# Weight sums, activation differences and output stores: three rearrangements in a fused attention and two-network kernel

## The chip, the cores and the metric

The kernel runs on one core of a Trainium2 chip. The metric is the device time of one launch in microseconds (us), as the median of several runs.

## The reference

```
a    = softmax(scale * q @ k^T, causal) @ v
mem  = (phi(q) @ M_prev) / (phi(q) . z_prev + 1e-6)      phi(x) = elu(x) + 1
x    = sigmoid(beta) * mem + (1 - sigmoid(beta)) * a     -> 2304 tokens x 512
h    = x @ moe_w_in            512 x 2048
x    = (h * cos(h)) @ moe_w_out
h    = x @ moe2_w_in
out  = (h * tanh(softplus(h))) @ moe2_w_out              -> 2304 x 512
```

Everything is float32, with 4 batches, 8 heads, 576 positions and 64 values a head. h * tanh(softplus(h)) is the Mish function.

## The kernel before

TensorE works on pairs of numbers: each float32 operand is split into a rounded upper half (H) and the remainder (L), and a product is three matmuls, H by H, H by L and L by H. Whoever makes an operand makes a rounded copy and then subtracts it from the original; that subtraction is called the remainder below.

The work has four stages. In the first, attention runs in 80 steps (batch, head pair, block of queries), and beside it the first half of the first network: products with w_in (L428) in 256 columns, the cosine, its remainders gL on Pool (L400), products with w_out (L494). The second stage, from some 405 us, is the second half of the first network with 512 columns. The third and last is the second network as a Strassen product: three blocks of 768 tokens, in each of them eight groups of 256 hidden units, so 24 groups. A group has seven products with w_in (`product`, L771) into three PSUM banks A, B, C, which are added up on the way: x1 is a copy of the first product by ScalarE (L786), `add` (L669, VectorE) adds x1 or a sum to a bank, `act` (L673, ScalarE) is Mish. From the four activations r11, r12, r21 and r22, `sub` makes four differences. `t1` and `t2` are new tiles and are made on VectorE (L662); the other two overwrite r12 and r21 in place and are made on Pool (L664), by the last group on VectorE. `halves` rounds each of the seven operands on ScalarE (L130) and makes its remainder on Pool (L680). `last_products` multiplies the operands of two groups at a time by sums of w_out (L744); `done` adds each to a sum in SBUF (L710), and at the last pair of groups of a token block combines the seven sums by additions that go to VectorE and Pool in turn (L704, L721) and stores the results (L708).

The Strassen network needs sums of weights, which `strassen_weights` makes for 16 pieces: sums and differences on Pool (L560), rounded copies on ScalarE (L130), remainders on Pool or VectorE in turn (L566) and a store to DRAM (L567). Six pieces are made beside attention, by a generator `gi` of which each attention step from 29 to 79 takes one turn. The other ten are made beside the second half of the first network by `gc`, one or two turns for each unit of that network; `strassen_x` makes sums of the input beside it in the same way (L584, L591, L605, L607). `load_w` (L620) brings the sums back, on the queue of SyncE (SP), where output stores are issued as well.

The program is written stage by stage. A scheduler of the language orders the instructions of each engine by its own estimate of the time; the engines then run in that order, each one waiting at an instruction until its operands are there. `tc.issue_after(x)` tells the scheduler that what follows may not be placed ahead of instruction x; `marks` holds the last instruction of a kind, and `TURNS` the engines that a kind of work goes to in turn ("p" Pool, "v" VectorE, "a" ScalarE).

```
halves(k, "S3", sub(r22, r12, r12, k + 1 == n))
halves(k, "A22", sub(t2, r21, r21, k + 1 == n))
...
with tc.issue_after(marks["cos"]), tc.issue_after(last_sin[0]):
    for _ in range(1 if i % SUM2 == 0 else 2):
        next(gc, None)
```

## Time and profile before

| | |
|---|---|
| runs shown | 1056.64, 1059.21, 1059.36 us, median 1059.21 |
| profiled execution | 1057.27 us, of which 1055.5 us are the span of the trace |
| granted TensorE clock, mean of the span | 0.986 |
| busy: TensorE, VectorE, ScalarE, Pool | 96%, 64%, 55%, 60% of the span |

The span runs from the first instruction to the last; busy time is the time in which an engine executes an instruction, so an engine that waits counts as idle. In rows of the trace PE is TensorE, DVE is VectorE, ACT is ScalarE, POOL is Pool and SP is SyncE, and L400 is line 400 of the kernel.

### The profile page before, as it was taken

The page shows a single profiled execution, that of the slowest core. Times are in us where ns is not written, and L with a number is a line of the kernel's source. Part 1 is how long each engine was busy: PE and PEld are TensorE (multiplying, and loading weights), DVE is VectorE, ACT ScalarE, POOL GpSimd, SP SyncE. Part 2 cuts the span into 40 slices and gives each one's busy share as a digit, 9 for nine tenths or more (in the row PEclk, how much of TensorE's full clock was granted, in tenths as well). Part 3 has the DMA queues.
Part 4 walks back from the last instruction along what each step waited for, and adds up shares of the span by engine and source line. Part 5 has one row for each costly group of instructions (what it writes and reads, how often), then busy time and mean ns, then how long its engine had stood idle before and what let it go on. Part 6 is the DMA issues. An engine that isn't in the chain of part 4 may idle for free.

```text
span 1055.5 us, 19374 instructions
## 1 busy us (share of the span) xinstructions
PE 1017.3 (96%) x6704; PEld 897.9 (85%) x6704; DVE 673.5 (64%) x1400; ACT 576.1 (55%) x1274; POOL 634.7 (60%) x623
## 2 busy tenths in 40 slices
PE   6998999999999999999999989998999999999997
PEld 4665678887878889998887878898999899999996
DVE  3589866667565645885495876453597347962557
ACT  5787576758576653334365555456444454445441
POOL 3368754454444533555386687279677767786664
PEclk8999799999999999999999999999999999999999
DMA  7377554636342247435268989996977888797882
GB/s 255 130 217 243 176 196 145 208 100 232 120 166 104 80 146 269 160 101 170 98 236 291 325 298 335 406 329 246 380 268 256 262 289 293 237 310 237 276 282 80
DMA packets 121841, 236.19 MB, mean 224 GB/s; under 512 B 11920, under 2 KB 35984, under 8 KB 121744
## 3 DMA queue, kind: packets, MB, share of 16 engines
q1 hardware_dynamic: 121744, 234.95, 65.2%
q8 instruction: 54, 0.88, 0.3%
q14 instruction: 43, 0.35, 0.1%
HBM read 176.44 MB, written 58.46 MB: 223 GB/s over the span
## 4 chain that ended last, share of the span: by engine, by line
PE 67%; DMA 9%; DVE 9%; ACT 6%; POOL 4%; issue 4%; SPq 1%; POOLq 0%; ACTq 0%; DVEq 0%
PE y L744 15%; PE h L771 15%; PE h L428 12%; PE y L494 11%; PE o L339 4%; PE sp L252 4%; PE tp L312 3%; DMA wst<-in_w1i_dram 2%; DMA wst<-in_w1o_dram 2%; PE o L328 1%; DVE wst L146 1%; DMA w<-woD 1%; DMA wsD<-ws 1%; POOL at L279 1%; DMA woD<-ws 1%
## 5 line engine op out<-in xcount | busy, mean ns | idle before, releaser
L494 PE MATMUL y<-g,w 128*128 128x256 f32 (+1 forms) x1344 | 222.4, 318 | 4.9 <-POOL g L400 3.9
L680 POOL TENSOR_TENSOR g<-us,g 128x384 fp32r<-128x384 f32 x164 | 177.3, 1099 | 74.2 <-ACT g L130 73.0
L494 PEld LDWEIGHTS y<-g,w 128*128 128x128 f32 x1344 | 191.3, 190 | 33.5 <-issue 10.3
L428 PE MATMUL h<-xbH,w 128*128 128x256 f32 (+1 forms) x896 | 206.5, 318 | 0.6 <-DMA xbH<-xsH 0.6
L744 PE MATMUL y<-g,w 128*128 128x384 f32 x1008 | 196.2, 336 | 4.0 <-DMA w<-woD 2.5
L771 PE MATMUL h<-xc,wq 128*128 128x384 f32 x1008 | 195.7, 335 | 2.6 <-ACT us L786 2.5
L279 POOL TENSOR_SCALAR at<-at,sm,omg 128x128 f32<-128x128 f32 (+2 forms) x144 | 114.3, 802 | 115.2 <-DVE sm L277 68.0
L744 PEld LDWEIGHTS y<-g,w 128*128 128x128 f32 x1008 | 175.9, 188 | 7.2 <-DMA w<-woD 2.4
L771 PEld LDWEIGHTS h<-xc,wq 128*128 128x128 f32 x1008 | 176.2, 188 | 3.4 <-ACT us L786 2.8
L400 POOL TENSOR_TENSOR g<-u,g 128x512 fp32r<-128x512 f32 x72 | 103.3, 1449 | 111.7 <-ACT g L130 54.5
L428 PEld LDWEIGHTS h<-xbH,w 128*128 128x128 f32 x896 | 151.3, 192 | 12.9 <-DMA xbH<-xsH 1.0
L428 PE MATMUL h<-xbL,w 128*128 128x256 f32 (+1 forms) x448 | 141.3, 316 | 0.0
L669 DVE TENSOR_TENSOR us<-h,us 128x384 f32<-128x384 f32 x120 | 66.3, 554 | 109.6 <-PE h L771 78.7
L130 ACT ACTIVATE g<-us 128x384 fp32r<-128x384 f32 x168 | 86.4, 523 | 57.1 <-DVE us L662 29.9
L428 PEld LDWEIGHTS h<-xbL,w 128*128 128x128 f32 x448 | 85.9, 192 | 5.3 <-issue 0.3
L673 ACT ACTIVATE us<-us 128x384 f32<-128x384 f32 x72 | 37.6, 524 | 96.1 <-DVE us L669 96.1
L257 ACT ACTIVATE at<-at,mn 128x128 f32<-128x128 f32 (+3 forms) x128 | 71.0, 556 | 26.1 <-DVE mn L254 24.4
L382 ACT ACTIVATE u<-h 128x512 int32<-128x512 f32 x72 | 42.0, 591 | 71.1 <-PE h L428 70.9
L710 DVE TENSOR_TENSOR ac<-y,ac 128x384 f32<-128x384 f32 x120 | 63.8, 550 | 22.1 <-PE y L744 21.7
L254 DVE CUSTOM_DVE_ANT_0 at<-sp,mask 128x128 f32<-128x128 f32 (+3 forms) x128 | 59.5, 483 | 25.5 <-PE sp L252 20.5
L312 PE MATMUL tp<-ident,at 128*128 128x128 f32 x384 | 65.5, 289 | 9.6 <-POOL at L279 6.0
L383 DVE SCALAR_TENSOR_TENSOR u<-u,h 128x512 f32<-128x512 int32 x72 | 48.3, 679 | 39.5 <-ACT u L382 39.4
(106 smaller groups left out, 1561.5 us busy)
## 6 DMA issues: line engine op xcount, KB each, us to landing
wq<-wsD SPq DMA_DIRECT2D x168, 256.0 KB, 4.5
w<-woD SPq DMA_DIRECT2D x168, 256.0 KB, 4.7
wsD<-ws SPq DMA_DIRECT2D x24, 512.0 KB, 3.2
woD<-ws SPq DMA_DIRECT2D x24, 512.0 KB, 4.4
wst<-in_w1i_dram SPq DMA_DIRECT2D x16, 512.0 KB, 4.5
wst<-in_w1o_dram SPq DMA_DIRECT2D x16, 512.0 KB, 4.8
wst<-in_w2i_dram SPq DMA_DIRECT2D x16, 512.0 KB, 4.5
wst<-in_w2o_dram SPq DMA_DIRECT2D x16, 512.0 KB, 5.2
```

Source lines behind the costliest of these rows:

```text
L130: eng.activation(dst, src, AF.Copy, scale=scale)
L257: marks["act"] = nc.scalar.activation(at[:, :N], at[:, :N], AF.Exp, bias=mn[:, j:j + 1], scale=-1.0, accum_out=sm[:, j:j + 1]).ins
L279: marks["pool"] = turn_of("sc", b == 0).tensor_scalar(at[:, :N], at[:, :N], sm[:, j:j + 1], gates[j], ALU.mult, ALU.mult).ins
L312: nc.tensor.transpose(tp[:, c:c + P], at[:, c:c + P], ident)
L400: turn_of(kind).tensor_tensor(gL, g, gH.bitcast(F32), ALU.subtract)
L428: nc.tensor.matmul(h[:, a * T:(a + 1) * T], w_[:, c, f0:f0 + P], x_[c], start=m == 0, stop=m == 3 * NC - 1)
L494: nc.tensor.matmul(y[e // per][:, cols], w_[:, f, es], g_, start=fst and m == 0 and e % per == 0, stop=lst and m == 2, skip_group_check=True)
L669: marks['v'] = nc.vector.tensor_tensor(c, b, x, ALU.add).ins
L680: ins = turn_of("ml" if k + 1 < n else "mz").tensor_tensor(t[:, 1], x, t[:, 0].bitcast(F32), ALU.subtract).ins
L710: marks['v'] = nc.vector.tensor_tensor(a, *((a, y) if less else (y, a)), ALU.subtract if less else ALU.add).ins
L744: nc.tensor.matmul(y, w_[:, wl, c], x[:, xl], start=m == 0, stop=m == 3 * KS - 1, skip_group_check=True)
L771: nc.tensor.matmul(b, w[name][:, wl, c], x[name][:, xl, c], start=first and m == 0, stop=m == 5, skip_group_check=True)
```

## The change

It makes five edits. (1) The turns of `gi` beside attention begin six steps later in the constant (SUM0 38, first turn at step 35), and every fifth step takes two. (2) `split` records its last remainder (L400), and the turns of `gc` are placed behind that one as well as behind the cosine. (3) `sub` makes all four differences on VectorE, so that 2 of each of 23 groups change engine. (4) Output stores go to a list, and are issued at the head of the chain of last products two turns later, in the last pair of groups at once. (5) The final sums of the last token block go to VectorE alone ("yz").

```diff
--- before.py
+++ after.py
@@ -25,7 +25,7 @@
 CONV0 = 14
 LOAD0 = 9
 AHEAD = 3
-SUM0 = 32
+SUM0 = 38
 SUMS = 6
 SUM2 = 3
 XSUM0 = 37
@@ -39,7 +39,7 @@
 TURNS = dict(
     sc0="p", aT0="a",
     sc="p", ws="p", w0l="pv", w1l="vp", w2l="vp", gl="p", gh="v", bh="a", mh="a",
-    wh="ap", aT="av", yl="p", ml="p", y0="v", y1="a", aD="v", y3="a", yf="vp", mz="vp", x3l="v", x3l0="pv", x3d0="p", x3d="v", ws4="p", ws2="a", wh2="a",
+    wh="ap", aT="av", yl="p", ml="p", y0="v", y1="a", aD="v", y3="a", yf="vp", yz="v", mz="vp", x3l="v", x3l0="pv", x3d0="p", x3d="v", ws4="p", ws2="a", wh2="a",
 )
 
 
@@ -397,7 +397,7 @@
         gg = wk.tile([P, 2, SM], F32R, tag="g", name="g", bufs=BUFS["g"])
         gH, gL = gg[:, 0], gg[:, 1]
         scaled(cast, gH, g)
-        turn_of(kind).tensor_tensor(gL, g, gH.bitcast(F32), ALU.subtract)
+        marks["gl"] = turn_of(kind).tensor_tensor(gL, g, gH.bitcast(F32), ALU.subtract).ins
         return gH, gL
 
     def units(blk, half):
@@ -644,6 +644,7 @@
         g = {}
         acc = {}
         w2 = {}
+        stores = []
         chain = [(k, name) for k in range(0, n, KS) for name in LAST]
         g3 = [wk.tile([P, 2, TS], F32R, tag=f"g3{i}", name="g3", bufs=1) for i in range(BUFS["g3"])]
         sums = [wk.tile([P, TS], F32, tag=f"ac{i}", name="ac", bufs=1) for i in range(14)]
@@ -655,13 +656,9 @@
         def cell():
             return wk.tile([P, TS], F32, tag="us", name="us", bufs=BUFS["us"])
 
-        def sub(x, y, out=None, vector=True):
-            if out is None:
-                out = cell()
-            if vector:
-                marks['v'] = nc.vector.tensor_tensor(out, x, y, ALU.subtract).ins
-            else:
-                marks['p'] = nc.gpsimd.tensor_tensor(out, x, y, ALU.subtract).ins
+        def sub(x, y, out=None):
+            out = cell() if out is None else out
+            marks['v'] = nc.vector.tensor_tensor(out, x, y, ALU.subtract).ins
             return out
 
         def add(b, x):
@@ -687,10 +684,10 @@
                 with tc.issue_after(marks["s"]):
                     w2[i] = [load_w(groups[k][1], name, "w2", woD) for k in range(k0, k0 + KS)]
 
-        def done(k0, name, c, y):
+        def done(turn, k0, name, c, y):
 
             t0, tl = groups[k0]
-            r = groups[k0][0]
+            turns = "yf" if t0 + 2 * TS < NT else "yz"
             if tl == 0:
                 a = acc[name, c] = sums[LAST.index(name) + 7 * c]
                 scaled("y3", a, y)
@@ -701,11 +698,11 @@
 
             def pre(n, other, op=ALU.add):
                 x = acc[n, c]
-                turn_of("yf").tensor_tensor(x, *((other, x) if op == ALU.subtract else (x, other)), op)
+                turn_of(turns).tensor_tensor(x, *((other, x) if op == ALU.subtract else (x, other)), op)
 
             def store(x, e, h):
                 e = (2 * e + c) * P
-                nc.sync.dma_start(out[e:e + P, t0 + h * TS:t0 + (h + 1) * TS], x)
+                stores.append((turn + 2, out[e:e + P, t0 + h * TS:t0 + (h + 1) * TS], x))
 
             marks['v'] = nc.vector.tensor_tensor(a, *((a, y) if less else (y, a)),
                                                  ALU.subtract if less else ALU.add).ins
@@ -718,7 +715,7 @@
                 store(a, 0, 0)
             elif name == "S2":
                 pre("S3", a)
-                turn_of("yf").tensor_tensor(a, a, acc["S1", c], ALU.add)
+                turn_of(turns).tensor_tensor(a, a, acc["S1", c], ALU.add)
                 pre("S4", a)
                 store(acc["S4", c], 0, 1)
             elif name == "S3":
@@ -734,6 +731,8 @@
             yield
             for i, (k0, name) in enumerate(chain):
                 fetch_last(i + 2)
+                while stores and stores[0][0] <= i:
+                    nc.sync.dma_start(*stores.pop(0)[1:])
                 ws = w2.pop(i)
                 xs = [g.pop((k, name)) for k in range(k0, k0 + KS)]
                 for c in range(2):
@@ -744,7 +743,9 @@
                             nc.tensor.matmul(y, w_[:, wl, c], x[:, xl], start=m == 0, stop=m == 3 * KS - 1,
                                              skip_group_check=True)
                             m += 1
-                    done(k0, name, c, y)
+                    done(i, k0, name, c, y)
+                    while stores and k0 + KS == n:
+                        nc.sync.dma_start(*stores.pop(0)[1:])
                     if c == 1:
                         free.extend(slot for slot, _ in xs)
                     yield
@@ -813,8 +814,8 @@
                 halves(k, "S1", t1)
                 t2 = sub(r22, t1)
                 halves(k, "S2", t2)
-                halves(k, "S3", sub(r22, r12, r12, k + 1 == n))
-                halves(k, "A22", sub(t2, r21, r21, k + 1 == n))
+                halves(k, "S3", sub(r22, r12, r12))
+                halves(k, "A22", sub(t2, r21, r21))
                 w = nw
                 if groups[k][1] == ng // 2 - 1 and k + ng < n:
                     nt = groups[k + ng][0]
@@ -866,7 +867,8 @@
                 converted(int((s - CONV0 + 1) * CONVR))
         if kind == "a" and s >= SUM0 - AHEAD:
             with tc.issue_after(marks["act"]), tc.issue_after(marks["pool"]), tc.issue_after(marks["vec"]):
-                next(gi, None)
+                for _ in range(2 if s % 5 == 0 else 1):
+                    next(gi, None)
         if kind != "c":
             continue
         b, r = divmod(s, steps_b)
@@ -906,7 +908,7 @@
                 break
             i += 1
             if done_b == 4 * NTL - 1:
-                with tc.issue_after(marks["cos"]), tc.issue_after(last_sin[0]):
+                with tc.issue_after(marks["cos"]), tc.issue_after(last_sin[0]), tc.issue_after(marks["gl"]):
                     for _ in range(1 if i % SUM2 == 0 else 2):
                         next(gc, None)
             if i >= XSUM0 and i % 2 == 1:
```

The scheduler turns these into other orders. The places below are those that the prediction speaks of; the numbers in names are the buffers'.

Pool, second half of the first network (g: remainders L400 of two tiles of one unit, u_7080; L605 and L566: input and weight sums), before:

```order
L400 TENSOR_TENSOR g_7116<-u_7080,g_7116 128x512
L605 TENSOR_TENSOR xr_7044<-xr_7048,xr_7044 128x768
L400 TENSOR_TENSOR g_7120<-u_7080,g_7120 128x512
L566 TENSOR_TENSOR ws_7010<-sw_6925,ws_7010 128x2x256
L560 TENSOR_TENSOR sw_7062<-wst_6810,wst_6901 128x256
```

and now:

```order
L400 TENSOR_TENSOR g_7116<-u_7080,g_7116 128x512
L400 TENSOR_TENSOR g_7120<-u_7080,g_7120 128x512
L605 TENSOR_TENSOR xr_7044<-xr_7048,xr_7044 128x768
L566 TENSOR_TENSOR ws_7010<-sw_6925,ws_7010 128x2x256
L560 TENSOR_TENSOR sw_7062<-wst_6810,wst_6901 128x256
```

The second remainder now stands ahead of the input sum. TensorE a little later (h: first products L428, y: second products L494), before:

```order
L428 MATMUL h_7299<-xbH_7087,w100_5114 128x512
L428 MATMUL h_7299<-xbL_7089,w100_5114 128x512
L428 MATMUL h_7299<-xbH_7087,w110_5115 128x512
L494 MATMUL y_7014<-g_7213,w123_5128 128x512
L494 MATMUL y_7015<-g_7213,w123_5128 128x512
L494 MATMUL y_7016<-g_7213,w123_5128 128x512
```

and now, where the rows are the last five of eight products into h_7382 and h_7405 and the first two of twelve into h_7270 and h_7299, behind which y_7014 comes:

```order
L428 MATMUL h_7382<-xbH_7083,w101_5118 128x512
L428 MATMUL h_7382<-xbL_7085,w101_5118 128x512
L428 MATMUL h_7382<-xbH_7083,w111_5119 128x512
L428 MATMUL h_7405<-xbH_7083,w101_5118 128x512
L428 MATMUL h_7405<-xbL_7085,w101_5118 128x512
L428 MATMUL h_7270<-xbH_7087,w100_5114 128x512
L428 MATMUL h_7270<-xbL_7089,w100_5114 128x512
```

Eight products of the next units, h_7382 and h_7405, now stand ahead of y_7014 that stood behind it.

The handover to the Strassen network on Pool (ws: weight remainders L566; sw: weight sums L560; g: remainders L400; g3: the Strassen network's remainders, L680 before and L677 now), before:

```order
L566 TENSOR_TENSOR ws_7341<-wst_7036,ws_7341 128x256
L400 TENSOR_TENSOR g_7724<-u_7688,g_7724 128x512
L400 TENSOR_TENSOR g_7728<-u_7688,g_7728 128x512
L400 TENSOR_TENSOR g_7844<-u_7808,g_7844 128x512
L400 TENSOR_TENSOR g_7848<-u_7808,g_7848 128x512
L566 TENSOR_TENSOR ws_7378<-sw_7292,ws_7378 128x2x256
L680 TENSOR_TENSOR g3_7862<-us_7935,g3_7862 128x384
L560 TENSOR_TENSOR sw_7433<-wst_7167,wst_7264 128x256
L560 TENSOR_TENSOR sw_7433<-wst_7167 128x256
L680 TENSOR_TENSOR g3_7863<-us_7970,g3_7863 128x384
L560 TENSOR_TENSOR sw_7433<-sw_7433,wst_7167 128x256
L560 TENSOR_TENSOR sw_7433<-wst_7264,sw_7433 128x256
```

and now:

```order
L400 TENSOR_TENSOR g_7632<-u_7596,g_7632 128x512
L566 TENSOR_TENSOR ws_7378<-sw_7292,ws_7378 128x2x256
L560 TENSOR_TENSOR sw_7433<-wst_7167,wst_7264 128x256
L560 TENSOR_TENSOR sw_7433<-wst_7167 128x256
L560 TENSOR_TENSOR sw_7433<-sw_7433,wst_7167 128x256
L560 TENSOR_TENSOR sw_7433<-wst_7264,sw_7433 128x256
L400 TENSOR_TENSOR g_7724<-u_7688,g_7724 128x512
L400 TENSOR_TENSOR g_7728<-u_7688,g_7728 128x512
L400 TENSOR_TENSOR g_7844<-u_7808,g_7844 128x512
L400 TENSOR_TENSOR g_7848<-u_7808,g_7848 128x512
L677 TENSOR_TENSOR g3_7862<-us_7935,g3_7862 128x384
L677 TENSOR_TENSOR g3_7863<-us_7970,g3_7863 128x384
```

One weight remainder and four weight sums now stand ahead of the last four L400, and none among the first L677. VectorE at the same place (us_8008 and us_7983 are r12 and r21, h are PSUM banks; the additions are L669 before and L666 now, the differences L662 and L661), before:

```order
L669 TENSOR_TENSOR us_8008<-h_7961,us_7913 128x384
L517 TENSOR_TENSOR yp_8189<-y_7855,yp_8189 128x512
L662 TENSOR_TENSOR us_8011<-us_8008,us_7935 128x384
L662 TENSOR_TENSOR us_8015<-us_7970,us_8011 128x384
L669 TENSOR_TENSOR us_8065<-h_8046,us_8055 128x384
L566 TENSOR_TENSOR ws_7502<-sw_7433,ws_7502 128x2x256
L517 TENSOR_TENSOR yp_8193<-y_7856,yp_8193 128x512
L669 TENSOR_TENSOR us_8099<-h_8046,us_8055 128x384
```

and now:

```order
L666 TENSOR_TENSOR us_8008<-h_7961,us_7913 128x384
L661 TENSOR_TENSOR us_8011<-us_8008,us_7935 128x384
L661 TENSOR_TENSOR us_8015<-us_7970,us_8011 128x384
L661 TENSOR_TENSOR us_8008<-us_7970,us_8008 128x384
L566 TENSOR_TENSOR ws_7502<-sw_7433,ws_7502 128x2x256
L661 TENSOR_TENSOR us_7983<-us_8015,us_7983 128x384
L666 TENSOR_TENSOR us_8065<-h_8046,us_8055 128x384
L666 TENSOR_TENSOR us_8099<-h_8046,us_8055 128x384
```

The differences that overwrite r12 and r21 now stand on VectorE, the second directly ahead of the next group's first addition.

SyncE's queue at the end of the first token block (L620: weight loads, w2 for `last_products` and wq for `product`; out: six of the block's eight stores, of which the first stands four loads further ahead before), before:

```order
L620 DMA w2_9535<-woD_62 128x512
L620 DMA w2_9537<-woD_62 128x512
L708 DMA out_0_dram<-ac_7882 128x384
L708 DMA out_0_dram<-ac_7885 128x384
L708 DMA out_0_dram<-ac_7892 128x384
L620 DMA wq_9554<-wsD_61 128x512
L708 DMA out_0_dram<-ac_7888 128x384
L620 DMA wq_9590<-wsD_61 128x512
L708 DMA out_0_dram<-ac_7889 128x384
L620 DMA wq_9600<-wsD_61 128x512
L620 DMA w2_9604<-woD_62 128x512
L620 DMA w2_9606<-woD_62 128x512
```

and now:

```order
L620 DMA w2_9531<-woD_62 128x512
L620 DMA w2_9533<-woD_62 128x512
L735 DMA out_0_dram<-ac_7881 128x384
L735 DMA out_0_dram<-ac_7882 128x384
L620 DMA wq_9551<-wsD_61 128x512
L735 DMA out_0_dram<-ac_7885 128x384
L735 DMA out_0_dram<-ac_7888 128x384
L735 DMA out_0_dram<-ac_7892 128x384
L620 DMA wq_9586<-wsD_61 128x512
L735 DMA out_0_dram<-ac_7889 128x384
L620 DMA wq_9596<-wsD_61 128x512
L620 DMA w2_9600<-woD_62 128x512
```

The first store moves behind four loads and two others behind one; the load of w2_9600, w2_9604 before, stands behind all six in both.

## Rows read from the trace of the kernel before

**Rows 1.** Page, busy time, share of the span and instructions of each engine.

```profile
PE 1017.3 (96%) x6704; PEld 897.9 (85%) x6704; DVE 673.5 (64%) x1400; ACT 576.1 (55%) x1274; POOL 634.7 (60%) x623
```

**Rows 2.** Windows: stretch, length, busy of PE, PEld, DVE, ACT, POOL, clock, DMA share, GB/s.

```profile
116.00:131.00 15.00, 14.18 (x117) 11.45 (x114) 11.96 (x29) 8.48 (x23) 9.41 (x12) 0.84 0.42 121
131.00:162.00 31.00, 30.44 (x239) 24.11 (x238) 20.12 (x69) 21.32 (x57) 17.49 (x21) 1.00 0.64 219
600.00:700.00 100.00, 96.10 (x524) 83.97 (x523) 63.10 (x76) 52.68 (x88) 62.90 (x49) 1.00 0.95 350
1000.00:1056.00 56.00, 47.62 (x270) 46.29 (x268) 36.00 (x62) 16.81 (x34) 30.39 (x29) 0.97 0.53 184
```

**Rows 3.** Waits of PE: line and what it waited for, us in total, times, longest.

```profile
PE y L494 <- POOL g L400: 3.9, 4, 1.7
PE y L744 <- DMA w<-woD: 2.5, 2, 2.1
```

**Rows 4.** Timeline of PE, 604 to 622: start, us, instructions [idle before <-releaser].

```profile
610.08 2.81 PE L494 MATMUL y<-g,w 128*128 128x512 f32 x11 [1.15 <-POOL g L400]
...
620.96 1.21 PE L494 MATMUL y<-g,w 128*128 128x512 f32 x4 [1.74 <-POOL g L400]
```

**Rows 5.** Timeline of POOL, 602 to 622.

```profile
605.77 2.57 POOL L605 TENSOR_TENSOR xr<-xr 128x768 f32<-128x768 f32 x1
608.31 1.71 POOL L400 TENSOR_TENSOR g<-u,g 128x512 fp32r<-128x512 f32 x1
...
616.88 2.35 POOL L584 TENSOR_TENSOR xc<-xr,xc 128x768 fp32r<-128x768 f32 x1 [1.08 <-ACT xc L583]
```

**Rows 6.** Timeline of PE, 678 to 730.

```profile
680.31 5.78 PE L494 MATMUL y<-g,w 128*128 128x256 f32 x46 [0.85 <-POOL g L400]
...
718.44 0.97 PE L744 MATMUL y<-g,w 128*128 128x384 f32 x4 [0.51 <-POOL g L680]
...
725.52 4.44 PE L771 MATMUL h<-xc,wq 128*128 128x384 f32 x24 [2.47 <-ACT us L786]
```

**Rows 7.** Timeline of POOL, 660 to 730.

```profile
678.98 2.53 POOL L400 TENSOR_TENSOR g<-u,g 128x512 fp32r<-128x512 f32 x2 [15.61 <-ACT g L130]
...
722.94 1.18 POOL L560 TENSOR_TENSOR sw<-wst,sw 128x256 f32<-128x256 f32 x1
```

**Rows 8.** Timeline of DVE, 715 to 730.

```profile
719.38 0.56 DVE L669 TENSOR_TENSOR us<-h,us 128x384 f32<-128x384 f32 x1 [4.30 <-POOL g L680]
722.38 1.15 DVE L566 TENSOR_TENSOR ws<-sw,ws 128x512 fp32r<-128x512 f32 x1 [2.43 <-ACT ws L130]
```

**Rows 9.** Groups by line, 700 to 1056: count | busy, mean ns | idle before.

```profile
L680 POOL TENSOR_TENSOR g<-us,g 128x384 fp32r<-128x384 f32 x161 | 173.7, 1097 | 72.1 <-ACT g L130 70.9 <-PE y L744 1.0
...
L669 DVE TENSOR_TENSOR us<-h,us 128x384 f32<-128x384 f32 x114 | 63.1, 555 | 101.6 <-PE h L771 74.7 <-POOL g L680 20.3 <-ACT ac L130 2.4
L664 POOL TENSOR_TENSOR us<-us 128x384 f32<-128x384 f32 x45 | 52.0, 1158 | 18.0 <-DVE us L662 14.7 <-PE y L744 2.7 <-DMA w<-woD 0.5
L662 DVE TENSOR_TENSOR us<-us 128x384 f32<-128x384 f32 x48 | 40.0, 836 | 7.9 <-ACT us L673 5.8 <-ACT ac L130 1.2
```

**Rows 10.** Waits of DVE: us in total, times, longest.

```profile
DVE us L669 <- POOL g L680: 20.3, 10, 4.3
```

**Rows 11.** Chain that ended last, 800 to 835: start, us, what.

```profile
826.40 5.84 DMA w<-woD
```

**Rows 12.** Timeline of all engines, 1040 to 1056.

```profile
1042.51 5.85 PE L744 MATMUL y<-g,w 128*128 128x384 f32 x32 [0.41 <-DVE g L680]
...
1044.24 1.48 DVE L710 TENSOR_TENSOR ac<-y,ac 128x384 f32<-128x384 f32 x3
...
1048.52 3.78 POOL L704 TENSOR_TENSOR ac<-ac 128x384 f32<-128x384 f32 x3 [0.49 <-DVE ac L721]
```

## The prediction

> **What bounds the kernel now.** I read the page's first rows: TensorE is busy for 1017.3 of 1055.5 us [rows 1], so a change on VectorE, Pool or SyncE's queue is worth only the TensorE idle time that it removes or adds. Next came the table by windows, which shows where the change can reach it. Beside attention, where the weight sums lie that come later, TensorE idles 0.82 us in 116 to 131 and 0.56 us in 131 to 162 (length minus PE's first number); in 600 to 700 it idles 3.9 us while the DMA engines are 0.95 busy; in 1000 to 1056 it idles 8.4 us [rows 2]. The table of waits then names what TensorE waits for after 405 us, where its matmuls are otherwise dense: 3.9 us for Pool's remainders of the first network's activations (L400), 2.5 us for a weight load (w from woD) [rows 3]; a further 2.5 us, for the copy x1 (L786), stands in [rows 6]. The timelines place these in six gaps that I call a to f:
> - a, 1.15 us, and b, 1.74 us: second half of the first network, both behind L400 [rows 4];
> - c, 0.85 us (L400), d, 0.51 us (L680), e, 2.47 us (L786): the handover to the Strassen network [rows 6];
> - f, 2.1 us: a weight load behind output stores [rows 3, 11].
>
> Together 8.8 us. The reader is to see why each arises. Gap a: Pool ran an input sum L605 (605.77, 2.57 us) before the remainder that TensorE wanted, which began at 608.31 [rows 5]. Gap b: L584 (616.88, 2.35 us) stood ahead of two remainders in the same way [rows 5]. Gap c: Pool had waited 15.61 us and began two remainders at 678.98, 1.3 us before TensorE went on [rows 7]. Gaps d and e: Pool was still making weight sums (L560, as at 722.94) between the remainders L680 [rows 7]; VectorE waited 4.30 us for such a remainder before an addition L669 and then 2.43 us for ScalarE before L566 [rows 8], and the copy that TensorE waited for was late with them.
>
> **The change, part by part.**
>
> *Weight sums of the second half wait for L400* (the new wait on marks["gl"]). In Pool's new order both remainders of u_7080 stand ahead of L605, so gap a goes: 1.15 us. At b Pool's order hardly changes, but TensorE has eight more first products ahead of the y that waited. Eleven 512-column matmuls take 2.81 us with the drain of the last one [rows 4], so at most 0.26 us each and 2.0 us for the eight, against a gap of 1.74; I take 1.5, since what feeds them may be late too. At c the products of 7663 and 7695 come first; I take 0.7 of 0.85. At d and e the remainder ws_7378 and four sums of sw_7433 move to where Pool idled 15.61 us [rows 7]; of 2.98 us I take 2.0, since the L566 and the rest of the L560 work of the last two pieces still stand among the remainders.
>
> What is queued behind the waiting sums: their own weight copies on ScalarE, the store of each piece, and then the loads of that piece by the Strassen network. Pool's 15.61 us of idle time before 678.98 [rows 7] is the cover; without it a late piece is a late weight load, in a stretch where the DMA engines are 0.95 busy [rows 2].
>
> *46 subtractions go from Pool to VectorE* (two of a group of 24, the last group had them there already). Pool is relieved of 45 recorded instructions of 1158 ns, 52 us; VectorE gets 46 x 836 ns = 38.5 us, by the mean of the same operation there [rows 9]. VectorE is 673.5 us busy of 1055.5, Pool 634.7 [rows 1], so neither becomes the bound as a mean. Both ran beside TensorE's products; taken by itself the move costs 0, covered by the next group's matmuls (24 in 4.44 us, 0.185 us each [rows 6]). The cover is gone where the second of the two subtractions, which overwrites r21, waits for Pool's remainder of r21, and the next group's first addition L669 is queued behind it on VectorE; before, that wait was Pool's own order and held up nothing of VectorE's. Its price is rival B.
>
> Here a rule stands against the change. The row shows: a subtraction of two SBUF tiles takes 836 ns on VectorE, an addition with one operand in PSUM (L669) 555 ns [rows 9], so some 0.28 us per instruction is lost to something. The Trainium skill, page "SBUF — State Buffer", section "Who interferes with whom", says that a VectorE instruction with two SBUF inputs contends with a Pool instruction that reads SBUF, because its second input comes through a read port that the two share. If each of the 46 waited for a whole remainder of Pool's, VectorE would pay 46 x (0.555 + 1.097) = 76 us by the durations of [rows 9] instead of 38.5, which by this estimate would be 3.3 us in a group instead of 1.7. The trace agrees in kind, 836 against 555 ns, not in the full size. My sum goes by the 836 ns.
>
> *Stores issued two turns later.* Gap f stands in the chain as a load of 5.84 us that ended at 832.24 [rows 11]. In SyncE's new order the next weight load for the last products (w2_9600, w2_9604 before) still stands behind all six stores; one store moves behind four loads, two behind one. So the part hardly does what it says. I take 0.5 of 2.1 us; the bounds are 0 and 2.1.
>
> *The final sums of the last block all on VectorE.* The end now is three Pool additions of 3.78 us from 1048.52 and a last VectorE addition to 1052.1, after TensorE's last 32 matmuls from 1042.51 [rows 12]. In the new order VectorE has 14 instructions in series after the S2 addition. That addition is the last of the three that end at 1045.72; three took 1.48 us, 0.49 each, and 14 more end at 1045.72 + 6.9 = 1052.6, against 1052.3 for Pool's last [rows 12]. I take 0; the bounds are 0.9 either way, from 0.43 to 0.56 us for each of the 14.
>
> *Weight sums beside attention nine steps later, two in some steps.* The same 48 steps of sums are done by step 76 instead of 79. TensorE idles 1.4 us in the whole stretch in which they lie [rows 2], so a gain is at most 1.4; a loss is a sum that delays Pool's scaling of attention where two come at once. I take 0 and bound the loss by 1.7 us, the longest wait for one Pool instruction in [rows 3]. The clock was 0.84 in 116 to 131 [rows 2]; nothing in the new order thins out TensorE there, so I leave it.
>
> *New gaps.* Every order so far left gaps of 0.5 to 2.5 us; I charge one of mean size for the new order, 8.8 / 6 = 1.5 us.
>
> **The sum.** -1.15 - 1.5 - 0.7 - 2.0 - 0.5 + 1.5 = -4.35 us. The profiled execution took 1057.27 us; 1057.27 - 4.35 = 1052.9. That execution stands 1.94 us under the median of the runs shown (1059.21) and 0.97 under the middle of all four times (1058.24); I add the 0.97: **1053.9 us**.
>
> **The rivals.**
>
> *A, the gaps only move.* For: the DMA engines are 0.95 busy from 600 to 700 [rows 2], none of the six gaps is longer than the 2.57 us of one L605 [rows 5], and a new order puts another long Pool instruction ahead of another remainder. Against: in the new order a and b are gone at their places. Then two new gaps of 1.5 us stand against the 4.35 + 1.5 = 5.85 us removed, and the stretch loses a further 1.5 us to late loads: 1058.24 - 5.85 + 4.5 = 1056.9, no change.
>
> *B, VectorE's queue turns over to Pool's pace: slower.* Place: the end of each group, where the subtraction into r21 waits on VectorE for Pool's remainder, and the next addition L669 waits behind it. For: VectorE already waited 20.3 us in 10 places for Pool's remainders before L669, at most 4.3 us [rows 10]; Pool's remainders are 161 of 1097 ns, seven in a group [rows 9]. Against: Pool loses its own two subtractions, 2.3 us of a group, so its remainder of r21 comes earlier. Cover: 18 matmuls, 18 x 0.185 = 3.3 us. A wait as long as the longest, 4.3 us, is 1.0 us over it. In half of the 23 groups that is 11.5 us; with a, b and c still gained (3.35) it gives 1058.24 + 11.5 - 3.35 = 1066.4. It decides from 7.6 us on (3.2 over the bound of no change and 4.35 that it eats up), 0.33 us of TensorE per group. The contention on the shared port would lengthen just this wait.
>
> *C, all gaps close.* All six, and the 1.4 us beside attention: 1058.24 - 8.8 - 1.4 = 1048.0. For: Pool has 52 us less to do. Against: f does not hang on Pool.
>
> *D, the stores part does not do what it says*: f stays whole; 1054.4, inside the forecast.
>
> **How the numbers follow.** Forecast with D 0.48, A 0.26, B 0.16, C 0.10. A measurement of this kernel can tell 0.3% from no change, 3.2 us: faster is below about 1055. Of the forecast's 0.48 I put 0.42 below it and 0.06 above, with C 0.10: faster 0.52; A and the 0.06: same 0.32; B: slower 0.16. Range: the low end is C less the 0.9 us of the tail, 1047; at the top A with the 1.7 us beside attention and the tail's 0.9 gives 1059.5, and the lower part of B, where few groups are late, takes it to 1061. What lies outside is most of B and a little of C. The forecast's own case is 1051 to 1057 (one new gap more or less, f whole or gone).
>
> **What would show it.** Right: TensorE's wait for L400 falls from 3.9 us to under 1; no wait for the copy x1 over 1 us near the handover; Pool's busy time falls to about 580 us and VectorE's rises to about 712; VectorE's mean for subtractions stays at 0.8 to 0.95 us. Wrong: TensorE waits for VectorE's additions L666 or the copy x1 in many groups (B); gaps of the same sum at other L494 or L428 places (A); attention ending over 1 us later. If TensorE's idle time after 405 us is unchanged or the clock row shows a stretch below 1.00 that was full before, the sum is wrong at its root.

## The result: slower by 0.6%

The changed kernel takes 1065.14 us (median of 8 runs, 1060.92 to 1069.69), the kernel before 1058.97 on the same chip (8 runs, 1056.50 to 1061.89). The ratio is 1.0059, 95% interval [1.0035, 1.0083]. The forecast was 1053.9, faster, so both its sign and its range were wrong; rival B had 1066.4. The profiled execution shown here took 1060.92 us with a span of 1059.0, the fastest of its eight, so the losses read from it are if anything small.

The page of the changed kernel, first rows (busy us, share of the span, instructions):

```profile
span 1059.0 us, 19383 instructions
...
PE 1016.4 (96%) x6704; PEld 896.3 (85%) x6704; DVE 706.5 (67%) x1453; ACT 576.9 (54%) x1274; POOL 586.7 (55%) x570
```

Against [rows 1] Pool lost 48.0 us and VectorE gained 33.0; forecast were some 55 and 38. The table of what TensorE waited for (us in total, times, longest), rows of the second half of the first network and of the Strassen network:

```profile
PE h L772 <- DVE us L666: 4.5, 3, 2.1
...
PE y L743 <- DMA w<-woD: 3.1, 5, 1.4
PE h L428 <- DMA xbH<-xsH: 2.4, 1, 2.4
...
PE h L772 <- ACT us L670: 1.2, 2, 0.9
...
PE y L494 <- POOL g L400: 0.7, 1, 0.7
```

The waits for L400 fell from 3.9 to 0.7 us [rows 3], and the 2.47 us for the copy x1 [rows 6] are gone. New are 4.5 us for VectorE's additions L666, which have no row in the list of before; the wait for a load of the first network's input grew from 0.6 to 2.4 us. Where this lies is seen by windows (stretch, length, busy of PE, PEld, DVE, ACT, POOL, clock, DMA share, GB/s). The kernel before:

```profile
700.00:800.00 100.00, 96.66 (x551) 94.96 (x550) 60.92 (x93) 52.82 (x108) 76.58 (x71) 1.00 0.83 292
800.00:840.00 40.00, 37.84 (x217) 37.22 (x216) 22.78 (x36) 17.76 (x38) 33.88 (x32) 1.00 0.85 276
840.00:925.00 85.00, 85.00 (x493) 85.00 (x492) 57.74 (x88) 41.91 (x84) 59.49 (x52) 1.00 0.80 269
925.00:960.00 35.00, 34.61 (x198) 33.99 (x197) 18.55 (x29) 17.55 (x37) 29.50 (x29) 1.00 0.90 299
```

and the changed one:

```profile
600.00:700.00 100.00, 95.15 (x523) 83.26 (x522) 64.10 (x78) 53.96 (x91) 65.17 (x52) 1.00 0.93 344
700.00:800.00 100.00, 98.43 (x567) 97.74 (x565) 72.32 (x108) 51.99 (x107) 62.21 (x56) 1.00 0.87 297
800.00:840.00 40.00, 36.34 (x205) 35.14 (x204) 24.68 (x38) 17.26 (x37) 24.69 (x22) 1.00 0.81 269
840.00:925.00 85.00, 83.59 (x478) 82.30 (x477) 62.37 (x97) 40.04 (x80) 49.53 (x42) 1.00 0.82 267
925.00:960.00 35.00, 32.50 (x179) 31.81 (x178) 23.88 (x34) 15.93 (x34) 23.27 (x22) 0.95 0.76 256
```

TensorE's idle time fell from 3.3 to 1.6 us in 700 to 800, the handover, and rose from 2.2 to 3.7, from 0 to 1.4 and from 0.4 to 2.5 in the three stretches behind it. In 600 to 700, where gaps a to c lay, it rose from 3.9 [rows 2] to 4.9. In the last stretch the mean clock was 0.95. TensorE had stood still for 2.14 us up to 943.16 and, six products later, for 0.36 us; from some 944.4 to 947.3 its granted clock then was 0.50, the lower of its two levels (1.2 instead of 2.4 GHz), and 1.00 again behind that. So this stretch lost some clock as well: it holds 179 products instead of 198.

The groups by line, 700 to 1060 (count | busy, mean ns | idle before), show what VectorE took over:

```profile
L677 POOL TENSOR_TENSOR g<-us,g 128x384 fp32r<-128x384 f32 x156 | 177.9, 1156 | 145.0 <-ACT g L130 114.7 <-PE y L743 13.3 <-issue 9.5
...
L661 DVE TENSOR_TENSOR us<-us 128x384 f32<-128x384 f32 x92 | 76.9, 867 | 9.2 <-ACT us L670 7.3
```

A difference takes 867 ns on average. By the trace, 19 of the 92 overlap no Pool instruction and take 555 ns on average; the 73 that do take 948, up to 1404. The kernel before shows the same two kinds: 8 of its 48 differences at 553 ns, 40 beside Pool at 893. The additions with one operand in PSUM take 552 ns either way, and Pool's remainder grew from 1097 [rows 9] to 1156 ns.

The chain that ended last, 812 to 834 (start, us, what), shows what a gap is made of:

```profile
815.07 1.37 DVE us L661
816.43 1.29 DVE ac L718
817.73 1.27 DVE ac L701
819.00 0.48 DVE us L666
819.48 0.04 issue
819.52 1.33 PE h L772 x6
...
823.32 0.38 SPq L620
...
823.76 5.22 DMA w<-woD
```

A difference and two final sums of the block, each of two SBUF tiles and each over twice its length alone, stand on VectorE ahead of the addition L666. TensorE's next product goes into the bank that this addition reads, and starts when it is done: a gap of 1.65 us. The second gap, 1.40 us before the products at 829.02, ends with the weight load of 5.22 us. On SyncE's queue this load stands behind the stores of the late sums, and behind a load whose buffer TensorE itself freed late, which is the way that the chain takes. It is the gap f of before, 2.1 us then.

### The profile page after: what moved, and what is told of

It reads as the page before. It is cut to its first block, busy times and chain, and to the rows that moved or that the text cites. A ratio compares the mean times of both kernels' runs of the same rounds, so it can differ in the third digit from the quotient of the medians.

```text
span 1059.0 us, 19383 instructions
## 1 busy us (share of the span) xinstructions
PE 1016.4 (96%) x6704; PEld 896.3 (85%) x6704; DVE 706.5 (67%) x1453; ACT 576.9 (54%) x1274; POOL 586.7 (55%) x570
## 4 chain that ended last, share of the span: by engine, by line
PE 71%; DMA 9%; DVE 7%; issue 5%; POOL 5%; ACT 2%; SPq 1%; DVEq 0%; POOLq 0%; ACTq 0%
PE h L772 14%; PE y L494 13%; PE y L743 13%; PE h L428 13%; PE o L339 5%; PE sp L252 4%; PE tp L312 4%; DMA w<-woD 2%; DMA woD<-ws 2%; DMA wst<-in_w2o_dram 2%; PE o L328 2%; PE mp L292 1%; POOL sw L560 1%; POOL g L400 1%; DVE us L661 1%
## 5 line engine op out<-in xcount | busy, mean ns | idle before, releaser
L677 POOL TENSOR_TENSOR g<-us,g 128x384 fp32r<-128x384 f32 x164 | 186.9, 1155 | 151.4 <-ACT g L130 119.4
L494 PE MATMUL y<-g,w 128*128 128x256 f32 (+1 forms) x1344 | 223.5, 319 | 3.7 <-ACT aT L130 1.6
L494 PEld LDWEIGHTS y<-g,w 128*128 128x128 f32 x1344 | 192.8, 192 | 31.8 <-issue 10.8
L428 PE MATMUL h<-xbH,w 128*128 128x256 f32 (+1 forms) x896 | 206.7, 316 | 3.4 <-DMA xbH<-xsH 2.4
L279 POOL TENSOR_SCALAR at<-at,sm,omg 128x128 f32<-128x128 f32 (+2 forms) x144 | 111.7, 784 | 105.3 <-DVE sm L277 84.0
L400 POOL TENSOR_TENSOR g<-u,g 128x512 fp32r<-128x512 f32 x72 | 103.2, 1448 | 116.9 <-ACT g L130 52.4
L428 PEld LDWEIGHTS h<-xbH,w 128*128 128x128 f32 x896 | 150.4, 190 | 16.4 <-DMA xbH<-xsH 2.6
L428 PE MATMUL h<-xbL,w 128*128 128x256 f32 (+1 forms) x448 | 140.6, 314 | 0.0
L666 DVE TENSOR_TENSOR us<-h,us 128x384 f32<-128x384 f32 x120 | 66.2, 553 | 92.1 <-PE h L772 83.5
L428 PEld LDWEIGHTS h<-xbL,w 128*128 128x128 f32 x448 | 85.2, 190 | 5.3 <-issue 0.3
L661 DVE TENSOR_TENSOR us<-us 128x384 f32<-128x384 f32 x96 | 80.2, 866 | 9.9 <-ACT us L670 8.0
```

What stands on the lines that cost most here:

```text
L279: marks["pool"] = turn_of("sc", b == 0).tensor_scalar(at[:, :N], at[:, :N], sm[:, j:j + 1], gates[j], ALU.mult, ALU.mult).ins
L400: marks["gl"] = turn_of(kind).tensor_tensor(gL, g, gH.bitcast(F32), ALU.subtract).ins
L428: nc.tensor.matmul(h[:, a * T:(a + 1) * T], w_[:, c, f0:f0 + P], x_[c], start=m == 0, stop=m == 3 * NC - 1)
L494: nc.tensor.matmul(y[e // per][:, cols], w_[:, f, es], g_, start=fst and m == 0 and e % per == 0, stop=lst and m == 2, skip_group_check=True)
L661: marks['v'] = nc.vector.tensor_tensor(out, x, y, ALU.subtract).ins
L666: marks['v'] = nc.vector.tensor_tensor(c, b, x, ALU.add).ins
```

## The experiments

All ratios are to the kernel before on the same chip. Its median differs from chip to chip, 1057.62 to 1061.45 us, so experiments are compared by their ratios. "V" marks a kernel with both differences on VectorE.

| kernel | median us | ratio, 95% interval |
|---|---|---|
| the change (V) | 1065.14 | 1.0059 [1.0035, 1.0083] |
| sub_undone | 1051.48 | 0.9934 [0.9911, 0.9958] |
| gi_undone (V) | 1063.31 | 1.0044 [1.0018, 1.0070] |
| gl_undone (V) | 1065.72 | 1.0061 [1.0035, 1.0087] |
| out_alone | 1063.08 | 1.0036 [1.0007, 1.0065] |
| yf_pool (V) | 1055.11 | 0.9976 [0.9953, 0.9998] |
| spare | 1065.01 | 1.0064 [1.0040, 1.0089] |
| a22_only | 1051.57 | 0.9931 [0.9905, 0.9957] |
| gl_gi | 1052.05 | 0.9925 [0.9900, 0.9950] |
| spare_ends | 1054.91 | 0.9936 [0.9913, 0.9959] |
| spare_mid | 1059.50 | 0.9995 [0.9971, 1.0020] |
| gi_alone | 1067.51 | 1.0071 [1.0043, 1.0098] |
| a22_yfp | 1051.48 | 0.9910 [0.9880, 0.9940] |
| spare_psum | 1054.92 | 0.9934 [0.9912, 0.9955] |
| spare_one | 1056.39 | 0.9956 [0.9935, 0.9978] |
| a22_no_gi | 1054.28 | 0.9934 [0.9905, 0.9964] |

**sub_undone: the two differences back on Pool, the rest of the change kept** (`sub` gets its two branches back).

```diff
-                halves(k, "S3", sub(r22, r12, r12))
-                halves(k, "A22", sub(t2, r21, r21))
+                halves(k, "S3", sub(r22, r12, r12, k + 1 == n))
+                halves(k, "A22", sub(t2, r21, r21, k + 1 == n))
```

> The change with two of the four differences of each group back on Pool. Theory V (the differences make VectorE's queue late at the ends of groups, and TensorE waits for an addition behind them): TensorE's waits for L666 and L670 (5.7 us together in the change) go below 1 us, and the time comes to 1055 to 1059 us, at or under the kernel before. Theory A (every build has its own order, and the new gaps are wherever its order puts a long instruction ahead of a short one): no fixed sign, anywhere from 1055 to 1066, with gaps of 20 to 25 us in sum after 405 us at other places. Theory G (the later weight sums beside attention cost it): 1064 to 1066, as the change.

It is 0.66% faster than the kernel before, where the change is 0.59% slower. Its 1051.48 us are less than any of the three theories had. So the differences cost 1.25%, 13 us, and the other four edits gain 7. The spans of the two traces differ by 5.4 us only, since the traced execution of sub_undone, 1055.38 us, comes 6.5 us later to the Strassen network. Within it the loss is whole. The rows are its products with w_in, the change first (ns min/median/max of one, then the first and the last start):

```profile
L772 PE MATMUL h<-xc,wq x1008: 333/334/686, 674.5 to 1039.1; 128*128 128x384 f32 x168
```

```profile
L776 PE MATMUL h<-xc,wq x1008: 334/334/440, 681.0 to 1033.6; 128*128 128x384 f32 x168
```

That is 364.6 against 352.6 us, a difference of 12.0. TensorE's waits after 700 us are down to these, the whole list:

```profile
PE y L747 <- POOL g L681: 0.8, 1, 0.8
PE y L747 <- DMA w<-woD: 0.8, 2, 0.4
```

and the stretches in which the change lost are full (idle 0, 0.4 and 0.7 us):

```profile
800.00:840.00 40.00, 40.00 (x232) 40.00 (x231) 22.93 (x37) 17.70 (x37) 32.76 (x31) 1.00 0.83 283
840.00:925.00 85.00, 84.65 (x488) 84.07 (x487) 58.68 (x86) 41.31 (x84) 60.91 (x53) 1.00 0.81 268
925.00:960.00 35.00, 34.32 (x195) 33.39 (x194) 19.37 (x29) 16.47 (x35) 27.90 (x27) 1.00 0.84 276
```

**gi_undone and gl_undone: the weight sums beside attention at their old steps; the wait on L400 taken out.**

```diff
-SUM0 = 38
+SUM0 = 32
...
-                for _ in range(2 if s % 5 == 0 else 1):
-                    next(gi, None)
+                next(gi, None)
```

```diff
-                with tc.issue_after(marks["cos"]), tc.issue_after(last_sin[0]), tc.issue_after(marks["gl"]):
+                with tc.issue_after(marks["cos"]), tc.issue_after(last_sin[0]):
```

> The change with the weight sums beside attention at their old steps. Theory V: as the change, 1063 to 1067, with TensorE's waits for L666 in the Strassen stage as in the change. Theory G: 1057 to 1060. Theory A: anywhere from 1055 to 1066.

> The change without the new wait of the second half's weight sums on Pool's remainders. Theory V: the Strassen stage as in the change and the second half of the first network 2 to 4 us longer, 1066 to 1070 in all. Theory A: anywhere from 1055 to 1066.

Neither differs from the change beyond its interval. So the later sums beside attention are not the loss. In the second, the waits for L400 are back:

```profile
PE y L494 <- POOL g L400: 5.3, 7, 1.8
```

but the time is not longer, and there the expectation missed: TensorE idles 1.4 us more than in the change in 405 to 600 and 1.5 more in 700 to 800, and 2.2 us less in 800 to 840. With both differences on VectorE, what the wait on L400 gains early is lost again later; that VectorE's queue is the reason was not tried here.

**out_alone, gl_gi and gi_alone: parts of the change on the kernel before** (the delayed stores and the last block's sums; both edits on weight sums; only the later ones beside attention).

> Only the delayed stores and the last block's final sums on VectorE, on the kernel before. Theory V: within 1 us of the kernel before in the Strassen stage. Theory T (the stores or the tail are the loss): 1062 to 1066. Theory A: 1055 to 1066.

> Only the two edits on the weight sums, on the kernel before: differences on Pool, stores at once, final sums of the last block in turn. If the delayed stores and the last block's sums on VectorE cost time as they do alone (3.8 us): 1046 to 1049. If they gain or do nothing once the weight sums wait: 1051 to 1055. If the weight sums are not what gained 8 us: 1057 to 1061.

> Only the later weight sums beside attention, on the kernel before. If the gain of the two edits on weight sums comes from the wait on L400 (six gaps after 405 us): within 3 us of the kernel before, with TensorE's waits for L400 at 3 to 6 us as there. If it comes from this edit: 1050 to 1054.

The two edits on weight sums give the whole gain of sub_undone, 0.75%; stores and last sums add nothing to it. Alone, stores and last sums measure 0.36% slower, in theory T's range and just clear of nothing, with the gaps at the handover still there (its wait for the copy x1 is 3.2 us); which of that is theirs was not tried. The later sums alone are 0.71% slower, which neither expectation had, by one gap: TensorE waits 9.0 us for a weight load that SyncE issues at 729.88. Ahead of it on SyncE's queue stand stores of weight sums (L567), one of which waited 9.9 us for a weight remainder (L566) that Pool made at 727, between the Strassen network's remainders and differences. The wait, and the chain's rows:

```profile
PE h L771 <- DMA wq<-wsD: 9.0, 1, 9.0
```

```profile
727.06 0.69 POOL ws L566
...
729.88 3.57 DMA wq<-wsD
```

Pool's last weight sum L560 starts at 728.7 us here, at 722.9 in the kernel before and at 708.5 in gl_gi. So the gain comes with the wait on L400, which moves this work of Pool's towards the head of the handover. The wait on L400 alone on the kernel before was not tried; a22_no_gi, below, has it without the later sums.

**yf_pool: the change, with the final sums of the first two blocks on Pool alone.**

```diff
-    ... yf="vp", yz="v", ...
+    ... yf="p", yz="v", ...
```

> The change with the final sums of the first two token blocks on Pool alone. Theory V1 (VectorE's queue is full where differences and final sums meet, at the ends of token blocks, and the addition L666 that TensorE needs stands behind them): the gaps of 1.8 and 2.3 us near 818 and 942 go, 1059 to 1062. Theory V2 (every group loses a little because its differences are on VectorE): 1064 to 1066.

14 of the 28 final sums (L701, L718) on VectorE go to Pool, and two thirds of the loss are gone (1.0059 to 0.9976), more than V1 expected. Pool has more to do than in the change, so it is not Pool's time that was short. The stretches of the block ends idle 1.9 and 0.3 us instead of 3.7 and 2.5:

```profile
800.00:840.00 40.00, 38.15 (x211) 37.83 (x210) 21.43 (x33) 17.89 (x37) 32.54 (x31) 0.96 0.81 270
...
925.00:960.00 35.00, 34.67 (x199) 34.20 (x199) 20.62 (x31) 17.38 (x37) 31.07 (x30) 1.00 0.84 286
```

**spare, and spare_psum: sub_undone with two more subtractions on VectorE in each of 23 groups, whose results nobody reads**; they write a tile of their own. In the first both operands lie in SBUF, in the second one is bank C in PSUM.

```diff
+                for x in (r22, t2):
+                    if k + 1 < n:
+                        marks['v'] = nc.vector.tensor_tensor(spare, x, t1, ALU.subtract).ins
```

```diff
+                for x in (r22, t1):
+                    if k + 1 < n:
+                        marks['v'] = nc.vector.tensor_tensor(spare, C, x, ALU.subtract).ins
```

> The kernel with the differences back on Pool (1051.5 us), and two spare differences of SBUF tiles on VectorE in each of 23 groups, whose results nobody uses. Theory V (VectorE's time is what costs): 1058 to 1066, with TensorE waiting for VectorE's additions as in the change. Theory L (what costs is that the operands S3 and A22 themselves come later from VectorE): 1051 to 1054.

> Two spare differences a group as before, but each with one operand in PSUM (bank C) and one in SBUF, so that Pool does not lengthen them. Theory P (what costs is that VectorE's instructions on two SBUF tiles grow to 1.2 us beside Pool): 0.55 us each, 1051 to 1056. Theory Q (two more instructions in VectorE's queue are what costs, at whatever length): 1060 to 1066. Between: 1056 to 1060, both count.

These two settle most. The spare ones with two SBUF operands cost 1.3%, as much as the moved ones, although no operand of TensorE comes from them: what costs is such work in VectorE's queue, not where S3 and A22 are made. With one operand in PSUM they cost nothing (0.9934 in both, without them and with them). Their group rows, the first with its engine idle before, the second likewise:

```profile
L824 DVE TENSOR_TENSOR spare<-us 128x384 f32<-128x384 f32 x45 | 52.3, 1163 | 0.2
```

```profile
L824 DVE TENSOR_TENSOR spare<-h,us 128x384 f32<-128x384 f32 x44 | 24.0, 546 | 0.0
```

The number of instructions is the same; one takes 1163 ns beside Pool, the other 546. From the first to the last product with w_in the first takes 366.6 us, the second 355.2, against 352.6 without spare ones. Pool's remainders are lengthened too, though little: 1148 ns in the first, 1119 in the second, 1116 without; and after 700 us TensorE waits for Pool in neither. What it waited for in the first is for the most part weight loads:

```profile
PE y L748 <- DMA w<-woD: 7.9, 6, 3.5
PE h L777 <- DVE us L671: 2.5, 3, 1.5
```

On SyncE's queue these loads stand behind the stores of VectorE's last sums and behind loads whose buffers TensorE frees; which of the two made each of them late was not separated.

**a22_only and spare_one: one difference a group on VectorE instead of two; one spare one instead of two.**

```diff
-                halves(k, "S3", sub(r22, r12, r12))
+                halves(k, "S3", sub(r22, r12, r12, k + 1 == n))
```

```diff
-                for x in (r22, t2):
+                for x in (t2,):
```

> The change with only the last difference of a group (into r21) on VectorE, the one into r12 on Pool. Theory V: between the two kernels, 1055 to 1061. Theory W (the wait of the r21 difference for Pool's remainder is the whole cost): as the change, 1063 to 1066.

> One spare difference of SBUF tiles a group instead of two. If the loss has a threshold, as one moved difference suggests: 1050 to 1055. If it is proportional to VectorE's added time: 1056 to 1060.

One moved difference costs nothing (0.9931 against 0.9934), which both expectations missed. One spare one costs 0.2%, not clear of nothing, since its interval overlaps that of sub_undone. Its 1056.39 us lie at the low end of the range given for a loss in proportion, but its ratio is clear of half of 1.3%. Two of either cost 1.3%: the loss grows faster than the number. The moved one is the one into r21, so rival B's wait is not the cost either. VectorE's busy time does not predict the loss: from 700 to 1040 it is 234 us of 340 in a22_only and 231 in the change.

```profile
700.00:1040.00 340.00, 337.03 (x1934) 334.61 (x1934) 234.42 (x355) 163.33 (x334) 225.90 (x200) 1.00 0.81 271
```

```profile
700.00:1040.00 340.00, 330.47 (x1879) 326.02 (x1878) 231.26 (x357) 159.28 (x326) 198.61 (x175) 0.99 0.80 268
```

The first row is a22_only, the second the change. What decides, as the gap at 819 us suggests, is what stands ahead of the addition when TensorE comes for its bank; that this is why one is free and two are not was not shown.

**spare_ends and spare_mid: the spare ones only in groups 8, 9, 16 and 17, beside the final sums; only in the others.**

```diff
-                    if k + 1 < n:
+                    if k in (8, 9, 16, 17):
```

```diff
-                    if k + 1 < n:
+                    if k + 1 < n and k not in (8, 9, 16, 17):
```

> The spare differences only in groups 8, 9, 16 and 17, eight instructions instead of 46, beside the final sums of the first two token blocks; the differences of the network on Pool. Theory V1 (the loss arises where differences and final sums meet on VectorE): 1055 to 1060, with TensorE idle 2 us or more in 800 to 840. Theory V2 (every group loses alike): 1052 to 1054.

> The spare differences in the other groups of the first 23, 38 instructions. Theory V1: 1052 to 1056, with 800 to 840 free of gaps. Theory V2: 1062 to 1065.

Theory V1 falls in its simple form, and V2 with it. Eight at the block ends cost nothing, 38 elsewhere half of the loss, and all 46 twice that, so the two don't add up. The stretch 800 to 840 idles 4.1 us with all, 0 with the ends alone and 1.1 with the rest alone; the rows are spare, spare_ends and spare_mid:

```profile
800.00:840.00 40.00, 35.87 (x196) 35.10 (x195) 31.98 (x43) 14.25 (x30) 34.10 (x30) 0.96 0.78 253
```

```profile
800.00:840.00 40.00, 40.00 (x233) 40.00 (x232) 27.49 (x37) 19.86 (x44) 31.70 (x30) 1.00 0.87 298
```

```profile
800.00:840.00 40.00, 38.89 (x223) 38.25 (x222) 23.30 (x38) 18.38 (x39) 31.03 (x29) 1.00 0.84 277
```

That the first block's end loses only where VectorE comes to it late already would fit these three and yf_pool. The second block's end does not bear it out: there spare_ends idles as much as the change, 2.5 us, without a loss in its median.

```profile
925.00:960.00 35.00, 32.50 (x186) 31.86 (x185) 22.45 (x32) 17.08 (x37) 26.56 (x24) 1.00 0.83 279
```

So it stays open why the parts don't add up; each build also has its own order, and each trace is of one execution.

**a22_yfp and a22_no_gi: a22_only with the final sums on Pool (the edit of yf_pool), and with the old steps of the sums beside attention (that of gi_undone).**

> The kernel with one difference a group on VectorE (1051.6 us), and the final sums of the first two blocks on Pool. If what is left in 800 to 960 hangs on VectorE: 1049 to 1051. If Pool, with 36 more us of work, is late in its place: 1053 to 1057.

> The kernel with one difference a group on VectorE (1051.6 us), with the weight sums beside attention at their old steps. If the later sums gain nothing, as the change with them undone says: 1050 to 1054. If they cost 7 us by themselves, as they did alone: 1043 to 1048. If they are half of the gain: 1055 to 1059.

The first has the lowest ratio of all, 0.9910, but its interval overlaps those of a22_only, gl_gi and sub_undone. Each of the four beats both kernels, and which is best can't be told. The second is no different from a22_only: once the wait on L400 is there, the later sums neither gain nor cost anything that can be measured.

## Why the prediction was wrong

- **The step that failed** is "taken by itself the move costs 0, covered by the next group's matmuls". It cost 13 us (sub_undone). The term's busy time was about right, 38.5 us forecast and 33.0 gained by the whole engine, and neither engine became the bound as a mean, as said. But the mean of 836 ns hid two kinds, 553 ns alone and 893 beside Pool (555 and 948 in the change), and I set the cover against one kind of wait only. The queue of VectorE at the end of a group holds four differences instead of two, at a block's end final sums as well, all with two operands in SBUF. One such difference a group more was covered, two were not; why the cover ends between them stays open.
- **The rule I weighed and set aside** is the one that the experiments bear out. The Trainium skill, page "SBUF — State Buffer", section "Who interferes with whom", has it that a VectorE instruction with two SBUF inputs contends with Pool's reads. The trace agrees, with spare_psum beside spare: 546 against 1163 ns for the same operation, and no loss against 1.3%. My estimate by it, 76 us for 46 differences, is too high: 46 x 867 ns are 40. Not each meets a whole instruction of Pool's; 19 of 92 met none.
- **Rival B** had the engine, the sign and the size, 1066.4 against 1065.14, from 11.5 us for the queue; that the size fits is luck. Its mechanism was wrong: VectorE's wait for Pool before the addition fell from 20.3 us in 10 places [rows 10] to 5.1 in 3, the list of VectorE's waits has none of a difference L661 for Pool's remainder, and the difference into r21 on VectorE alone cost nothing. The row of VectorE's waits in the change:

```profile
DVE us L666 <- POOL g L677: 5.1, 3, 3.6
```

- **The other edits** were forecast at -4.35 us and gave -7 (sub_undone, 0.66%). Gaps a, b, c and e closed as said: L400 3.9 to 0.7 us, no wait for x1. But a to c gained nothing: in 405 to 700 TensorE idles 4.7 us before, 4.9 in the change and 5.5 in sub_undone, since other gaps opened there, as rival A had it. The gain lies behind 700 us, where up to 1040 sub_undone idles 1.9 us and the kernel before 6.2. Gap f is 1.4 us instead of 2.1, and the end, from TensorE's last product on, is 7.5 us in both traces, as the 0 for the last block's sums has it. The new gap that I charged at 1.5 us is there: the wait for a load of the first network's input is 1.8 us longer in the change. That the stores part hardly does what it says (rival D) held: with the weight sums' edits it moved nothing, 0.9934 with and 0.9925 without. The edit beside attention was taken at 0 and is 0 with the wait on L400, but 7.5 us slower without it, by a gap at the handover that my bound of 1.7 us did not see, since I looked for its cost beside attention only. (That part says nine steps later; the first turn comes six later, 35 for 29, and no term of the sum hangs on it.)
- **The chances** gave 0.16 to slower. The row that should have raised it stood in the evidence: a difference whose length depends on Pool, in the one queue that TensorE's banks wait for.

## What to carry to other kernels

Before moving an elementwise operation to VectorE, look at where its operands lie, and cost it by the mean of those instances that ran beside Pool, not by the mean of all. Then look at what stands behind it in that queue: TensorE waits for the instruction that frees its bank, and each long instruction ahead of that one is on its path once the slack is gone, although the engine is 67% busy. Where two operands in SBUF can't be avoided, share them out between the two engines (three differences a group on VectorE and one on Pool were as good as two and two; four on VectorE were not), or take other work of the kind, such as the final sums, off the engine that feeds the banks.

## What was not expected of the hardware

Two subtractions of 128x384 of SBUF tiles in each of 23 groups, added with nobody reading them, cost the kernel 1.3%, and the same two with one operand in PSUM nothing that can be measured: 1163 against 546 ns each. And edits did not add up: the later weight sums alone cost 0.7%, and nothing once the wait on L400 is there; the wait on L400 showed no gain while both differences were on VectorE (1.0061 without it, 1.0059 with it), and the two edits on weight sums without them gained 0.75%.
